# Four PSUM banks in place of two for the block products of the last second-layer stage

## The chip, the cores and the metric

The kernel runs on one core of one Trainium2 chip. TensorE (PE) multiplies and writes its results to the accumulation memory PSUM; the kernel's two pools there divide it into eight banks of 512 fp32 values in each of 128 partitions. In the part that matters, VectorE (DVE) and ScalarE (ACT) read PSUM, GpSimd (POOL) works on the memory SBUF, and SyncE (SP) issues the output stores. The metric is the device time of one execution in microseconds; three runs of the kernel before gave 546.70, 546.79 and 546.79, median 546.79.

## What is computed

```python
attn = np.maximum(q @ k.T * scale, 0) ** 2 / S       # 8 batches, 12 heads, 448 x 64
x    = (attn @ v), heads side by side                # 8 x 448 x 768
xn   = (x - mean(x)) / sqrt(var(x) + 1e-6) * g_ln
out  = x + maximum(xn @ w_ch1, 0) @ w_ch2            # w_ch1: 768 x 3072, w_ch2: 3072 x 768
```

Inputs and output are fp32; the kernel multiplies in bf16 and accumulates in fp32. The division by the square root is done at the very end: each row of the second layer's result is multiplied by its 1/sqrt and x is added.

## The kernel before, in words

The eight batches are worked in four pairs of two batches, that is 896 tokens or seven tiles of 128 tokens a pair. For the first three pairs attention of the next pair is interleaved with the two layers of this one. The program is written out in order by hand (`manual_schedule`, L74): each engine executes its instructions in the order in which the Python code issues them, and semaphores are put in for every dependence between engines. For the waits, the unit in PSUM is the tile that a pool hands out.

The change lies in the last stage alone: the second layer of the last pair (L854 to L859). Here the hidden activations `h` (`hT`, bf16, 24 chunks of 128 by 896) and the weights `w2` are treated as 2 x 2 blocks. The two rows of blocks of `h` are the token tiles t and t+4, its two columns the halves of the 24 chunks; the blocks of `w2` are the halves of its chunks by the halves of its 768 columns. Seven block products in place of eight give the four results (a scheme of Strassen's kind). A product (`product(n)`, L706) is 12 matmuls, each 128x128 weights by 128x384 moving data, accumulated in one PSUM bank. Its left factor is `s3` or `s4` (parts of `hT`) or one of the sums of blocks of `h` (`s2`, `s5`, `s1`, `s6`, `s7`: `h_sums_of`, L685), its right factor one of the sums of blocks of `w2`, made earlier.

`ffn2_pair` (L699) does one pair of tiles and is called for t = 0, 1, 2; `ffn2_last` (L760) then does tile 3 in the ordinary way: 24 matmuls into a bank for its first 384 columns and 24 into a bank for each of two groups of 192 columns. In `ffn2_pair`:

- the products come in the order 3, 2, 5, 4, 1, 6, 7. Products 3 and 2 start in fresh banks `a` and `b`; 5 adds to `a` and 4 adds to `b`. Products 1 and 6 start in fresh banks again, and 7 adds to that of product 1. A fresh bank is a one-bank tile from the pool `ps_mm` (L90), which has two buffers; so product 1 uses the bank that 3 and 5 had, and 6 the bank of 2 and 4;
- between the products the intermediate values are read: ACT copies `a` to `d` (L733), DVE subtracts `b` from `d` (L735), ACT copies the sums `c12` (L738) and `c21` (L742), DVE makes `q_ = a + d` (L745), POOL takes `c12` from `d` and adds `c21` (L746, L747), DVE adds `b` to `q_` (L752) and the last `a` to `d` (L757);
- `result` (L720) multiplies a result by 1/sqrt and adds x, on DVE in one instruction (L724) or on ACT (L727) and POOL (L728), and issues two stores on SP (L645);
- `following` (L855) issues the sums of `h` for the next t on DVE: `s2` and `s5` in one instruction (L691), `s1` (L693), `s6` (L695) and `s7` (L697). For t = 2 it issues nothing.

On DVE the order for one t is then L735, L691, L745, L724 twice (`c12`, `c21`), L693, L752, L695, L697, L757, L724 (`d`). The other pool in PSUM, `ps_sc` (L89), has three buffers of two banks each, `[128, 2, 512]` fp32; it served attention and is idle in this stage.

Of the kernel before, what the change touches and what calls it, by code (L numbers as in the profile page):

```python
# [28 lines left out]
def kernel(  # L29
# [22 lines left out]
    nc = tc.nc  # L52
    P = 128
    HP = 64
    bf16 = mybir.dt.bfloat16
    fp32 = mybir.dt.float32
# [13 lines left out]
    DH = d_model // 2  # L70
# [18 lines left out]
    ps_sc = ctx.enter_context(tc.tile_pool(name="ps_sc", bufs=3, space=bass.MemoryType.PSUM))  # L89
    ps_mm = ctx.enter_context(tc.tile_pool(name="ps_mm", bufs=2, space=bass.MemoryType.PSUM))  # L90
# [550 lines left out]
    def store(pair, t, cols, o, queues):  # L641
        for u, queue in enumerate(queues):
            b, j = divmod(2 * t + u, J)
            rows = out[2 * pair + b].rearrange("(p j) d -> j p d", j=J)[j]
            queue.dma_start(rows[:, cols], o[u * HP:(u + 1) * HP])  # L645
# [39 lines left out]
    def h_sums_of(pair, t, names, lo, hi):  # L685

        h = hT[pair].rearrange("p (kh k) (u s) -> p kh k u s", kh=2, s=P)
        a = {(i, j): h[:, j, lo:hi, t + 4 * i] for i in range(2) for j in range(2)}
        if "s2" in names:
            two = [h[:, j, lo:hi, t:t + 5:4].rearrange("p k u s -> p u k s") for j in range(2)]  # L690
            nc.vector.tensor_add(h_sum["s25"][:, ::-1, lo:hi], *two)  # L691
        if "s1" in names:
            nc.vector.tensor_add(h_sum["s1"][:, lo:hi], a[0, 0], a[1, 1])  # L693
        if "s6" in names:
            nc.vector.tensor_sub(h_sum["s6"][:, lo:hi], a[1, 0], a[0, 0])  # L695
        if "s7" in names:
            nc.vector.tensor_sub(h_sum["s7"][:, lo:hi], a[0, 1], a[1, 1])  # L697

    def ffn2_pair(pair, t, late, following):  # L699


        h = hT[pair].rearrange("p (kh k) (u s) -> p kh k u s", kh=2, s=P)
        left = dict(h_sum, s3=h[:, 0, :, t], s4=h[:, 1, :, t + 4])
        left["s2"], left["s5"] = h_sum["s2"], h_sum["s5"]

        def product(n, ps=None):  # L706
            first = ps is None
            if first:
                ps = ps_mm.tile([P, 512], fp32, tag="mm", name="m_ps")
            x, y = left[f"s{n}"], w2_sum[f"t{n}"]  # L710
            for ki in range(KH):
                nc.tensor.matmul(ps[:, :DH], x[:, ki], y[:, ki],  # L712
                                 start=(first and ki == 0), stop=(ki == KH - 1),
                                 skip_group_check=not first)
            return ps

        def fp():
            return late.tile([P, DH], fp32, tag="z", name="z_sb", bufs=5)

        def result(eng, z, row, half):  # L720
            u = t + 4 * row
            z3, x = z.rearrange("p (c d) -> p c d", d=D), xtok[pair][:, :, u, half * HP:(half + 1) * HP]
            if eng is nc.vector:
                eng.scalar_tensor_tensor(  # L724
                    z3, z3, rstd[pair][:, u:u + 1], x, op0=ALU.mult, op1=ALU.add)
            else:
                nc.scalar.mul(z, z, rstd[pair][:, u:u + 1])  # L727
                eng.tensor_add(z3, z3, x)  # L728
            store(pair, u, slice(half * DH, (half + 1) * DH), z, (nc.sync, nc.sync))

        a = product(3)
        d = fp()
        nc.scalar.copy(d, a[:, :DH])  # L733
        b = product(2)
        nc.vector.tensor_sub(d, d, b[:, :DH])  # L735
        product(5, a)
        c12 = fp()
        nc.scalar.copy(c12, a[:, :DH])  # L738
        product(4, b)
        following("s2")  # L740
        c21 = fp()
        nc.scalar.copy(c21, b[:, :DH])  # L742
        a = product(1)
        q_ = fp()
        nc.vector.tensor_add(q_, a[:, :DH], d)  # L745
        nc.gpsimd.tensor_sub(d, d, c12)  # L746
        nc.gpsimd.tensor_add(d, d, c21)  # L747
        result(nc.vector, c12, 0, 1)
        result(nc.vector, c21, 1, 0)
        b = product(6)  # L750
        following("s1")
        nc.vector.tensor_add(q_, q_, b[:, :DH])  # L752
        result(nc.gpsimd, q_, 1, 1)
        product(7, a)
        following("s6")
        following("s7")
        nc.vector.tensor_add(d, d, a[:, :DH])  # L757
        result(nc.vector, d, 0, 0)

    def ffn2_last(pair, t):  # L760
# [93 lines left out]
    for t in range(3):  # L854
        def following(name, t=t):  # L855
            if t < 2:
                h_sums_of(pair, t + 1, (name,), 0, KH)
        ffn2_pair(pair, t, late, following)
# [31 lines left out]
```

## Time and profile before

| what | value |
|---|---|
| median of three runs | 546.79 us |
| the profiled execution | 546.87 us |
| its span, first to last instruction | 545.0 us |
| mean granted TensorE clock | 0.999 |
| PE busy, of the span | 533.3 us (98%) |
| DVE, ACT and POOL busy | 300.2, 267.9 and 119.6 us |
| first matmul of this stage (L712) starts | 487.69 us |
| first matmul of `ffn2_last` (L766) starts | 533.29 us |
| last instruction on DVE (L634) starts | 541.35 us |

A timeline view lists instructions in order of time: start, duration, engine, line, operation, output and inputs, how many were merged (`x12`), and in brackets how long the engine had been idle before and what ended that. A merged row of 12 matmuls is one product; `x24` is two products without a pause, `x36` three. A row of matmuls lasts until the modelled end of its last matmul, which is some 0.16 us after the next one may begin; so what matters is from start to start. The waits view gives, for each pair of waiter and releaser, the total in us, the number of times and the longest.

### The profile page before, as it was taken

Reading aid. Unit: us, or ns where it says so; the run is one execution under the profiler, and the core shown is the slowest. Engines: PE = TensorE matmul, PEld = TensorE weight load, DVE = VectorE, ACT = ScalarE, POOL = GpSimd, SP = SyncE. Lnnn points to the kernel's source line nnn. Section 1 sums busy time; section 2 is a strip of 40 time slices with the busy share of each in tenths; the row PEclk is TensorE's granted clock in tenths of the full one; section 3 lists DMA queues with packets and bytes.
Section 4 is the critical chain, followed back from the end, with each engine's and each line's share of the span. In section 5 each row is a group of like instructions: output and inputs, shape, how many; then the busy total and the mean of one; then the engine's idle time right before and its main releaser. Section 6 shows DMA issues by size and latency. Waiting matters only on the chain.

```text
span 545.0 us, 11195 instructions
## 1 busy us (share of the span) xinstructions
PE 533.3 (98%) x4720; PEld 315.5 (58%) x4720; DVE 300.2 (55%) x559; ACT 267.9 (49%) x440; POOL 119.6 (22%) x144
## 2 busy tenths in 40 slices
PE   8999999999999999999999999999999999999996
PEld 6677779655555555555555555555555555555555
DVE  5765752378886250057787432026687689035543
ACT  6967685555553444455545344445545244441110
POOL 7344111123526100003634400001230400001121
PEclk9999999999999999999999999999999999999999
DMA  9999999979999930029989980004831140001123
GB/s 197 206 205 208 211 171 185 168 126 160 164 152 146 167 42 1 0 55 147 163 149 134 176 109 1 1 14 88 151 75 31 44 102 1 1 0 26 34 58 88
DMA packets 111300, 56.64 MB, mean 104 GB/s; under 512 B 77330, under 2 KB 111250, under 8 KB 111250
## 3 DMA queue, kind: packets, MB, share of 16 engines
q0 software_dynamic: 26976, 25.50, 32.4%
q1 hardware_dynamic: 83490, 29.77, 31.8%
q8 instruction: 37, 0.61, 0.5%
q10 hardware_dynamic: 784, 0.66, 0.4%
q14 instruction: 13, 0.11, 0.1%
HBM read 51.91 MB, written 11.01 MB: 115 GB/s over the span
## 4 chain that ended last, share of the span: by engine, by line
PE 91%; DVE 2%; DMA 2%; POOL 2%; issue 1%; ACT 1%; POOLq 0%; DVEq 0%
PE h_ps L586 39%; PE o_ps L623 31%; PE sc_ps L331 7%; PE av_ps L361 6%; PE m_ps L712 5%; DMA w<-in_moe_w_ch_dram 2%; PE o_ps L766 1%; PE h_ps L608 1%; PE sum_ps L414 1%; DVE z_sb L724 1%; POOL z_sb L746 1%; ACT early L342 1%; PE tr_ps L216 0%; DVE h_sum L697 0%; POOL v_sb L126 0%
## 5 line engine op out<-in xcount | busy, mean ns | idle before, releaser
L586 PE MATMUL h_ps<-xc_sb,w 128*128 128x448 bf16 (+2 forms) x1368 | 218.9, 318 | 0.6 <-ACT early L342 0.3
L586 PEld LDWEIGHTS <-w 128*128 128x128 bf16 x1368 | 128.6, 98 | 86.6 <-issue 3.0
L623 PE MATMUL o_ps<-w,hT_sb 128*128 128x384 bf16 x1008 | 172.6, 326 | 0.0
L342 ACT ACTIVATE attn_sb<-sc_ps 128x896 bf16<-128x896 f32 (+4 forms) x150 | 126.4, 902 | 87.9 <-PE sc_ps L331 71.4
L594 ACT ACTIVATE hT_sb<-h_ps 128x448 bf16<-128x448 f32 (+2 forms) x213 | 103.0, 484 | 122.2 <-PE h_ps L586 121.7
L623 PEld LDWEIGHTS <-hT_sb 128*128 128x128 bf16 x1008 | 94.9, 98 | 74.7 <-issue 15.2
L344 DVE TENSOR_TENSOR attn_sb<-attn_sb 128x896 bf16<-128x896 bf16 x126 | 81.7, 654 | 40.2 <-ACT attn_sb L342 38.9
L565 DVE BATCH_NORM_STATS2 stats<-xtok_sb 128x6 f32<-128x384 bf16 x56 | 27.5, 533 | 34.3 <-DMA xtok_sb<-xT_sb 34.3
L397 POOL TENSOR_TENSOR part_sb<-part_sb,xT_sb 128x448 f32<-128x448 f32 x24 | 29.5, 1229 | 69.9 <-DVE xT_sb L368 62.3
L394 POOL TENSOR_TENSOR part_sb<-xT_sb 128x448 f32<-128x448 bf16 x6 | 6.6, 1105 | 172.9 <-DVE xT_sb L368 142.5
L571 DVE RECIPROCAL rstd_sb<-rstd_sb 128x1 f32<-128x1 f32 (+1 forms) x10 | 1.7, 168 | 72.4 <-ACT rstd_sb L570 72.4
L420 DVE SCALAR_TENSOR_TENSOR xc_sb<-total_sb,g_mean,xc_sb 128x448 bf16<-128x448 f32 (+2 forms) x54 | 29.0, 604 | 21.5 <-ACT total_sb L418 21.5
L634 DVE SCALAR_TENSOR_TENSOR o_sb<-o_ps,rstd_sb,xtok_sb 128x384 f32<-128x384 f32 (+1 forms) x45 | 27.0, 601 | 17.2 <-PE o_ps L623 11.0
L331 PE MATMUL sc_ps<-qT_sb,kT_sb 64*64 64x448 bf16 x504 | 35.0, 358 | 0.0
L368 DVE TENSOR_SCALAR xT_sb<-av_ps 128x896 bf16<-128x896 f32 (+2 forms) x30 | 27.0, 900 | 10.0 <-PE av_ps L361 9.8
L361 PE MATMUL av_ps<-attn_sb,v_sb 64*64 64x448 bf16 (+2 forms) x672 | 32.3, 327 | 0.0
L361 PEld LDWEIGHTS <-v_sb 64*64 64x64 bf16 x840 | 22.7, 107 | 11.9 <-issue 1.6
L384 DVE TENSOR_SCALAR xc_sb<-xT_sb,g_sb 128x448 bf16<-128x448 bf16 (+2 forms) x54 | 27.9, 567 | 1.0
L712 PEld LDWEIGHTS <-h_sum 128*128 128x128 bf16 x180 | 17.6, 98 | 12.9 <-issue 1.4
L331 PEld LDWEIGHTS <-kT_sb 64*64 64x64 bf16 x504 | 12.1, 105 | 17.6 <-issue 13.3
L126 POOL DMA_DIRECT2D v_sb<-in_v_dram x24 | 17.5, 730 | 20.2 <-PE av_ps L361 16.7
L746 POOL TENSOR_TENSOR z_sb<-z_sb 128x384 f32<-128x384 f32 x3 | 3.0, 998 | 81.7 <-DVE z_sb L745 81.7
(88 smaller groups left out, 335.8 us busy)
## 6 DMA issues: line engine op xcount, KB each, us to landing
out_dram<-o_sb SPq DMA_DIRECT2D x85, 96.0 KB, 3.0
v_sb<-in_v_dram POOLq DMA_DIRECT2D x24, 224.0 KB, 4.9
w<-in_moe_w_ch_dram POOLq DMA_DIRECT2D x12, 384.0 KB, 13.9
w<-in_moe_w_ch_dram POOLq DMA_DIRECT2D x4, 1152.0 KB, 20.0
q_sb<-in_q_dram POOLq DMA_DIRECT2D x20, 224.0 KB, 7.0
k_sb<-in_k_dram POOLq DMA_DIRECT2D x20, 224.0 KB, 5.7
out_dram<-z_sb SPq DMA_DIRECT2D x24, 96.0 KB, 2.2
hold_sb<-in_q_dram POOLq DMA_DIRECT2D x3, 224.0 KB, 11.9
```

Source lines behind the costliest of these rows:

```text
L331: nc.tensor.matmul(ps[cols, r, o * w:(o + 1) * w], g["k"](i)[rows, cols], g["q"](i, r)[rows, blk[0]:sum(blk), cols], start=True, stop=True)
L342: nc.scalar.activation(a, ps[:, :, :len(slots) * w], ACTF.Relu)
L344: nc.vector.tensor_mul(a, a, a)
L361: nc.tensor.matmul(ps[cols, hh, :w], v_sb[rows, pr, j * D:(j + 1) * D], g["attn"][i][rows, r, :], start=(j == 0), stop=(j == J - 1))
L384: nc.vector.tensor_scalar_mul(y, x, g_sb[:, c:c + 1])
L397: nc.gpsimd.tensor_add(part[b], part[b], x[:, c])
L420: nc.vector.scalar_tensor_tensor(xc[b][:, c, of(blk)], total, g_mean[:, c:c + 1], xc[b][:, c, of(blk)], op0=ALU.mult, op1=ALU.add)
L565: nc.vector.bn_stats(stats[:, n], xtok[pair][:, n * G:(n + 1) * G, t, :])
L586: nc.tensor.matmul(ps[:, :w], w1[:, c, ni * P:(ni + 1) * P], xc[b][:, c, of(blk)], start=(c == 0), stop=(c == K1 - 1))
L594: nc.scalar.activation(hT[pair][:, ni, o:o + w], ps[:, :w], ACTF.Relu)
L623: nc.tensor.matmul(ps[:, :DH], hT[pair][:, ki, t * P:(t + 1) * P], w2[:, ki, cols], start=(ki == 0), stop=(ki == K2 - 1))
L712: nc.tensor.matmul(ps[:, :DH], x[:, ki], y[:, ki], start=(first and ki == 0), stop=(ki == KH - 1), skip_group_check=not first)
```

## The change

The products' banks come from `ps_sc`: `banks()` takes one two-bank tile and hands out its halves as `a` and `b`. Each call of `ffn2_pair` takes two such tiles, the first for products 3, 2, 5 and 4, the second for 1, 6 and 7. The order of the products is the same. On DVE, the sums of `h` and the reads of banks move ahead of the results: after the change the order is L736 (was L735), L691, L747 (was L745), L693, L752, L695, L724 twice, L758 (was L757), L697, L724. The stores of `q_` are issued ahead of those of `c12` and `c21`. All lines below L705 shift by one or two.

```diff
-        def product(n, ps=None):
-            first = ps is None
-            if first:
-                ps = ps_mm.tile([P, 512], fp32, tag="mm", name="m_ps")
+        def banks():
+            two = ps_sc.tile([P, 2, 512], fp32, tag="sc", name="m_ps")
+            return two[:, 0, :DH], two[:, 1, :DH]
+
+        def product(n, ps, first=True):
             x, y = left[f"s{n}"], w2_sum[f"t{n}"]
             for ki in range(KH):
-                nc.tensor.matmul(ps[:, :DH], x[:, ki], y[:, ki],
+                nc.tensor.matmul(ps, x[:, ki], y[:, ki],
                                  start=(first and ki == 0), stop=(ki == KH - 1),
                                  skip_group_check=not first)
-            return ps
...
-        a = product(3)
+        a, b = banks()
+        product(3, a)
         d = fp()
-        nc.scalar.copy(d, a[:, :DH])
-        b = product(2)
-        nc.vector.tensor_sub(d, d, b[:, :DH])
-        product(5, a)
+        nc.scalar.copy(d, a)
+        product(2, b)
+        nc.vector.tensor_sub(d, d, b)
+        product(5, a, False)
         c12 = fp()
-        nc.scalar.copy(c12, a[:, :DH])
-        product(4, b)
+        nc.scalar.copy(c12, a)
+        product(4, b, False)
         following("s2")
         c21 = fp()
-        nc.scalar.copy(c21, b[:, :DH])
-        a = product(1)
+        nc.scalar.copy(c21, b)
+        a, b = banks()
+        product(1, a)
         q_ = fp()
-        nc.vector.tensor_add(q_, a[:, :DH], d)
+        nc.vector.tensor_add(q_, a, d)
         nc.gpsimd.tensor_sub(d, d, c12)
         nc.gpsimd.tensor_add(d, d, c21)
+        following("s1")
+        product(6, b)
+        nc.vector.tensor_add(q_, q_, b)
+        result(nc.gpsimd, q_, 1, 1)
+        following("s6")
         result(nc.vector, c12, 0, 1)
         result(nc.vector, c21, 1, 0)
-        b = product(6)
-        following("s1")
-        nc.vector.tensor_add(q_, q_, b[:, :DH])
-        result(nc.gpsimd, q_, 1, 1)
-        product(7, a)
-        following("s6")
+        product(7, a, False)
+        nc.vector.tensor_add(d, d, a)
         following("s7")
-        nc.vector.tensor_add(d, d, a[:, :DH])
         result(nc.vector, d, 0, 0)
```

## The prediction, written before the changed kernel ran

> **What bounds the kernel now.** I read the page first: it says which engine has no room.
>
> ```profile
> span 545.0 us, 11195 instructions
> PE 533.3 (98%) x4720; PEld 315.5 (58%) x4720; DVE 300.2 (55%) x559; ACT 267.9 (49%) x440; POOL 119.6 (22%) x144
> ```
>
> PE is the bound over the whole span, so only what makes PE wait, or stop waiting, can move the time. The second view is the list of waits, for PE alone, from 487 us on, where the changed lines run.
>
> ```profile
> PE m_ps L712 <- DVE z_sb L752: 2.5, 2, 1.3
> PE m_ps L712 <- DVE z_sb L757: 0.8, 1, 0.8
> PE o_ps L766 <- DVE z_sb L752: 0.4, 1, 0.4
> ```
>
> PE waits four times here, always for DVE to finish reading a bank (a fifth, short one shows below). The third view is the timeline of PE alone over the stage; the start of each row is what counts.
>
> ```profile
> 487.69 2.11 PE L712 MATMUL m_ps<-w_sum,hT_sb 128*128 128x384 bf16 x12
> 489.64 4.06 PE L712 MATMUL m_ps<-w,h_sum 128*128 128x384 bf16 x24
> 493.54 2.11 PE L712 MATMUL m_ps<-w_sum,hT_sb 128*128 128x384 bf16 x12
> 495.49 6.01 PE L712 MATMUL m_ps<-w_sum,h_sum 128*128 128x384 bf16 x36
> 502.74 2.11 PE L712 MATMUL m_ps<-w_sum,hT_sb 128*128 128x384 bf16 x12 [1.23 <-DVE z_sb L752]
> 505.66 4.06 PE L712 MATMUL m_ps<-w,h_sum 128*128 128x384 bf16 x24 [0.81 <-DVE z_sb L757]
> 509.55 2.11 PE L712 MATMUL m_ps<-w_sum,hT_sb 128*128 128x384 bf16 x12
> 511.50 6.01 PE L712 MATMUL m_ps<-w_sum,h_sum 128*128 128x384 bf16 x36
> 518.81 2.11 PE L712 MATMUL m_ps<-w_sum,hT_sb 128*128 128x384 bf16 x12 [1.29 <-DVE z_sb L752]
> 521.01 4.06 PE L712 MATMUL m_ps<-w,h_sum 128*128 128x384 bf16 x24
> 526.86 6.01 PE L712 MATMUL m_ps<-w_sum,h_sum 128*128 128x384 bf16 x36
> 533.29 8.02 PE L766 MATMUL o_ps<-w,hT_sb 128*128 128x384 bf16 x72 [0.42 <-DVE z_sb L752]
> ```
>
> A product that nothing holds up takes 1.95 us from start to start (487.69 to 489.64; 509.55 to 511.50), and the seven of one t run without a pause. The pauses lie between one t and the next. The fourth view is the timeline of all engines: when a bank's reader starts after a product.
>
> ```profile
> 504.88 0.48 ACT L733 COPY z_sb<-m_ps 128x384 f32<-128x384 f32 x1 [1.55 <-PE m_ps L712]
> 507.87 0.56 DVE L735 TENSOR_TENSOR z_sb<-z_sb,m_ps 128x384 f32<-128x384 f32 x1 [1.61 <-PE m_ps L712]
> 509.80 0.48 ACT L738 COPY z_sb<-m_ps 128x384 f32<-128x384 f32 x1 [4.43 <-PE m_ps L712]
> 513.71 0.56 DVE L745 TENSOR_TENSOR z_sb<-m_ps,z_sb 128x384 f32<-128x384 f32 x1 [2.20 <-PE m_ps L712]
> ```
>
> Product 3 starts at 502.74 and its reader, ACT's copy, at 504.88: 2.14 us later, more than the 1.95 after which PE could go on. So whenever the next product must await the reader of this one, PE loses the difference, the reader's own time and the release.
>
> **The change part by part.**
>
> *Removed: the waits between one t and the next.* With two one-bank buffers product 3 of the next t writes the bank that L752 read, and product 2 the bank that L757 read; both reads stand on DVE behind L724 and the sums of h. After the change these two products have a fresh two-bank tile out of three; its earlier readers were done a whole t before, and o_ps finds ps_mm empty. Loss now, from start to start: after three products from 495.49 (5.84 us) product 3 could start at 501.33 and starts at 502.74, 1.41; product 2 at 504.69 against 505.66, 0.97; then 517.34 against 518.81, 1.47; 520.76 against 521.01, 0.25; and o_ps at 532.70 against 533.29, 0.59. Sum **4.69 us removed**. The new order on DVE (bank reads and sums ahead of L724) would shorten the same waits; with fresh banks it has nothing left to gain, and I count it at nothing.
>
> *Added: waits inside each t.* The diff alone doesn't tell this; the order of the changed program's instructions with their waits does. For t = 1, the first matmul of each product (3, 2, 5, 4, 1, 6, 7, and then 3 of t = 2):
>
> ```
> 8956 L713 Matmult m_ps_6736<-w2_sum_6153,hT_sb_6154 128x384
> 8980 L713 Matmult m_ps_6736<-w2_971,h_sum_6546 128x384 [waits Activation_49]
> 9004 L713 Matmult m_ps_6736<-w2_971,h_sum_6546 128x384 [waits DVE_49]
> 9028 L713 Matmult m_ps_6736<-w2_sum_6153,hT_sb_6154 128x384 [waits Activation_49]
> 9052 L713 Matmult m_ps_6793<-w2_sum_6153,h_sum_6546 128x384
> 9076 L713 Matmult m_ps_6793<-w2_sum_6153,h_sum1_6547 128x384 [waits DVE_49]
> 9100 L713 Matmult m_ps_6793<-w2_sum_6153,h_sum1_6548 128x384 [waits DVE_49]
> 9124 L713 Matmult m_ps_6852<-w2_sum_6153,hT_sb_6154 128x384
> ```
>
> Both banks are one tile (m_ps_6736) now. Product 2 goes into a bank that nobody has used for a whole t, and yet waits for ACT: the semaphore's count is the one that L734 raises, ACT's copy of the *other* bank. In the same way 5 awaits DVE's read of b (L736), 4 ACT's copy of a (L739), 6 DVE's read of a (L747) and 7 DVE's read of b (L752). The dependence is kept by tile, and each of these readers reads the product just before. So five of the seven products start only when their predecessor has been finished, read out and released. Behind each waiting matmul stands all the rest of PE's queue, and nothing else bounds the end.
>
> The price of each is start to reader, plus the reader, plus the release, less 1.95. The release of PE by DVE: L752 ends at 502.14 + 0.54 = 502.68 and PE starts at 502.74, 0.06. By ACT no row of this stage has it; the nearest is at the kernel's start, where a copy (L342) ends at 12.63 and PE starts at 12.65: 0.02, and another there gives about 0.11. I take 0.05, near DVE's 0.06.
> - 3 to 2: 2.14 (504.88 - 502.74) + 0.48 + 0.05 - 1.95 = 0.72.
> - 2 to 5: 2.21 (507.87 - 505.66) + 0.56 + 0.06 - 1.95 = 0.88.
> - 5 to 4: product 5 starts 1.95 after 505.66, at 507.61; 2.19 (509.80 - 507.61) + 0.48 + 0.05 - 1.95 = 0.77.
> - 1 to 6: 2.21 (513.71 - 511.50) + 0.56 + 0.06 - 1.95 = 0.88.
> - 6 to 7: L752 never follows its product at once now, as L724 is ahead of it; with the readers' 2.14 to 2.21, so 2.18, + 0.54 + 0.06 - 1.95 = 0.83.
>
> Sum 4.08 a t, and three t: **12.2 us added**. From the ends of the rows (ACT's release 0.02 or 0.11; start to reader 2.14 or 2.22) a t costs 3.8 to 4.3, so 11.5 to 12.9.
>
> *Covers.* The price holds if the reader is free when its product ends. DVE's next reader is L747, behind L691 (1.76 us), which starts when product 5 ends; products 4 and 1 then take over 4 us. L752 stands behind L693 (0.87), beside product 6 (2.15). L736 of the next t stands behind L695, L724 twice, L758, L697 and L724; after product 7 only L758 (0.54), L697 (0.87) and L724 (0.62) are left, 2.0 us, beside products 3 and 2 of the next t, 4.8 us. ACT's L739 awaits a buffer that is stored behind L752, L727 (0.62) and L728 (1 to 1.7) of the t before, and such a store lands 2.2 us (median) after its issue: some 5 us after L752, while L739 comes over 9 us after it. If such a cover were gone, PE would wait the excess, once per t. L724's results come some 2 us later and the stores on SP in another order: nothing but the buffers awaits them. The tail after o_ps (541.32 to the end) is as before.
>
> **Sum.** The profiled execution took 546.87 us, 1.87 more than its span; it lies 0.08 above the median of the runs. + 12.2 - 4.7 = + 7.5 us: 546.79 + 7.5 = **554.3 us**, 1.4% slower.
>
> **The rivals.**
>
> *The added waits do not bite* (each bank waits for its own readers only). Then true dependences remain: 5 must await the copy of a, ready 2.7 us after product 3 starts, needed after 3.9; 4 and 7 likewise. Nothing stalls, only the 4.7 us go: 546.79 - 4.7 = 542.1, faster. For it: in the trace of before product 2 starts at 489.64 and writes its bank while ACT reads the other from 489.89, without a pause. It decides if what 8980 awaits were an older count of ACT than the copy's. Against it: the count is that of the copy just before, the same pattern stands in all three t, and fresh tiles (8956, 9052) have no wait at all. Chance 4%. The Trainium skill, PSUM — Partial Sum Buffer, section "PSUM bank collisions raise a hardware error", states that two engines on different banks run clean; by that the chip asks for none of the five waits, and the time would be this rival's 542.1. The trace agrees about the chip, at 489.64 and 489.89; but the waits are in the program, and PE executes them.
>
> *The clock falls.* Fifteen pauses of 0.8 us might let the granted clock drop. If one product of seven then ran at half speed, 1.95 us more per t, 5.9: 560.2. Against it: 1.41 us and 0.97 us lost within 4 us before 505.66 left the next 24 matmuls at 3.89 us, and the granted clock of the windows from 487.4 to 532.6 is 1.00. Chance 3%. The Trainium skill, TensorE: Matmul & The Clock Gate, section "A second HAM failure mode: psum-queue depth-cycling", tells of a kernel whose short idle times between groups in PSUM brought the clock down again and again; by it this rival would be the forecast, and no row here bears it out.
>
> **How the numbers follow.** Forecast 92%, no waits 4%, clock 3%; 1% that part of the hand-off is hidden and gain and loss cancel within 0.2%, which is about what a measurement of this kernel can tell from no change. Slower 95%, the same 1%, faster 4%. The range: + 11.5 - 4.7 gives 553.6, + 12.9 - 4.7 gives 555.0; 0.6 below and 1.0 above for the row that is not measured by itself (L752) and what a cover may cost: 553.0 to 556.0. The rivals lie outside, 8%.
>
> **What would show it.** Right: five pauses on PE in each t, 0.7 to 0.9 us each from start to start, ended by ACT L734 and L739 and by DVE L736, L747 and L752; none before product 1, before product 3 of the next t and before o_ps. PE's last matmul some 7.5 us later than before. Wrong: x36 rows without a pause in a t (first rival), or rows of 12 matmuls longer than 2.11 (second).

## The result, and the profile after

Four runs of the changed kernel gave 553.92 to 554.40 us, median 554.24, against 546.75 of four runs before: ratio 1.0137, interval 1.0119 to 1.0155. It is slower by 7.5 us. The profiled execution took 554.22 us, its span is 552.4, 7.4 longer than before. In four of the sets of runs below, and in one set of the kernel before, one run lies about 3 us above the others; the ratios take it in, the medians hardly do, so the text goes by medians.

The list of waits of PE from 487 us on, in the kernel after (waiter, releaser: us in total, times, longest):

```profile
PE m_ps L713 <- DVE z_sb L736: 2.1, 3, 0.7
PE m_ps L713 <- DVE z_sb L747: 1.9, 3, 0.6
PE m_ps L713 <- DVE z_sb L752: 1.9, 3, 0.6
PE m_ps L713 <- ACT z_sb L739: 1.8, 3, 0.6
PE m_ps L713 <- ACT z_sb L734: 1.7, 3, 0.6
```

The four waits of before are gone and five others are there, each once in each of the three t. The timeline of PE in the same kernel, for the second t and the start of the third, and the first row of `ffn2_last`:

```profile
505.46 2.11 PE L713 MATMUL m_ps<-w_sum,hT_sb 128*128 128x384 bf16 x12
508.14 2.11 PE L713 MATMUL m_ps<-w,h_sum 128*128 128x384 bf16 x12 [0.57 <-ACT z_sb L734]
510.97 2.11 PE L713 MATMUL m_ps<-w,h_sum 128*128 128x384 bf16 x12 [0.71 <-DVE z_sb L736]
513.69 2.11 PE L713 MATMUL m_ps<-w_sum,hT_sb 128*128 128x384 bf16 x12 [0.61 <-ACT z_sb L739]
515.63 2.11 PE L713 MATMUL m_ps<-w_sum,h_sum 128*128 128x384 bf16 x12
518.40 2.11 PE L713 MATMUL m_ps<-w_sum,h_sum 128*128 128x384 bf16 x12 [0.65 <-DVE z_sb L747]
521.15 2.11 PE L713 MATMUL m_ps<-w_sum,h_sum 128*128 128x384 bf16 x12 [0.64 <-DVE z_sb L752]
523.10 2.11 PE L713 MATMUL m_ps<-w_sum,hT_sb 128*128 128x384 bf16 x12
...
540.72 8.02 PE L768 MATMUL o_ps<-w,hT_sb 128*128 128x384 bf16 x72
```

The rows of 24 and 36 matmuls have fallen apart into single products. Products 3 (505.46, 523.10) and 1 (515.63) follow without a pause, as does `o_ps`; the other five each begin 2.7 to 2.8 us after the product before. From 487.83 to 540.72 the 21 products took 52.9 us where 21 x 1.95 = 40.9 would do: 11.9 lost. Before it was 45.6 (487.69 to 533.29), 4.7 lost. The difference of 7.3 us, and 0.14 by which the stage began later, is the whole of the 7.4.

### The profile page after: what moved, and what is told of

Read it like the earlier page. It is cut to its first block, busy times and chain, and to the rows that moved or that the text cites. A ratio compares the mean times of both kernels' runs of the same rounds, so it can differ in the third digit from the quotient of the medians.

```text
span 552.4 us, 11193 instructions
## 1 busy us (share of the span) xinstructions
PE 535.3 (97%) x4720; PEld 315.6 (57%) x4720; DVE 298.6 (54%) x559; ACT 267.9 (48%) x440; POOL 119.5 (22%) x144
## 4 chain that ended last, share of the span: by engine, by line
PE 93%; DMA 2%; POOL 1%; ACT 1%; DVE 1%; issue 1%; ACTq 0%; DVEq 0%; POOLq 0%
PE h_ps L586 39%; PE o_ps L623 31%; PE m_ps L713 8%; PE sc_ps L331 7%; PE av_ps L361 6%; DMA w<-in_moe_w_ch_dram 2%; PE o_ps L768 1%; PE h_ps L608 1%; PE sum_ps L414 1%; ACT early L342 1%; PE tr_ps L216 0%; POOL v_sb L126 0%; POOL w L144 0%; DVE z_sb L747 0%; DVE z_sb L752 0%
## 5 line engine op out<-in xcount | busy, mean ns | idle before, releaser
L342 ACT ACTIVATE attn_sb<-sc_ps 128x896 bf16<-128x896 f32 (+4 forms) x150 | 126.3, 902 | 87.4 <-PE sc_ps L331 70.9
L748 POOL TENSOR_TENSOR z_sb<-z_sb 128x384 f32<-128x384 f32 x3 | 4.2, 1385 | 92.2 <-DVE z_sb L747 92.2
L713 PE MATMUL m_ps<-w_sum,h_sum 128*128 128x384 bf16 x108 | 19.0, 326 | 3.9 <-DVE z_sb L747 1.9
L331 PEld LDWEIGHTS <-kT_sb 64*64 64x64 bf16 x504 | 12.1, 105 | 17.6 <-issue 13.3
## 6 DMA issues: line engine op xcount, KB each, us to landing
hold_sb<-in_q_dram POOLq DMA_DIRECT2D x3, 224.0 KB, 11.9
```

The costliest lines, as they stand in the source:

```text
L331: nc.tensor.matmul(ps[cols, r, o * w:(o + 1) * w], g["k"](i)[rows, cols], g["q"](i, r)[rows, blk[0]:sum(blk), cols], start=True, stop=True)
L342: nc.scalar.activation(a, ps[:, :, :len(slots) * w], ACTF.Relu)
L713: nc.tensor.matmul(ps, x[:, ki], y[:, ki], start=(first and ki == 0), stop=(ki == KH - 1), skip_group_check=not first)
```

## The experiments

The theory is the prediction's: dependences in PSUM are kept by tile, and with two banks in a tile a product awaits the reader of the product just before. Rivals are that the chip itself holds a product up while another bank is read, that two-bank tiles cost as such, and that the order on DVE matters by itself. Of the seven kernels below, the first, second, fourth and sixth stand beside eleven runs of the kernel before (median 546.81), the third and the seventh beside thirteen on another chip (546.83), the fifth beside ten (546.89).

**Four banks, each in its own tile** (the same order on every engine as in the changed kernel):

```diff
         def banks():
-            two = ps_sc.tile([P, 2, 512], fp32, tag="sc", name="m_ps")
-            return two[:, 0, :DH], two[:, 1, :DH]
+            a = ps_sc.tile([P, 2, 512], fp32, tag="sc", name="m_ps")
+            b = ps_mm.tile([P, 512], fp32, tag="mm", name="n_ps")
+            return a[:, 0, :DH], b[:, :DH]
```

> The changed kernel with a and b in tiles of their own (a from ps_sc, b from ps_mm): four banks as before, the same order on every engine. Theory, that the five waits a t come from two banks sharing a tile: all fifteen pauses go, PE runs from 488 us to its last matmul without one, 554.2 - 12.1 (measured loss from start to start in the changed kernel) = 542.2 us, 4.6 under the kernel before. Rival, that a product into a bank is held up on the chip itself while another bank is read: the pauses stay, 554 us.

Measured: 542.18 us. PE's timeline in this kernel, the last three products of the first t, the first of the next and `ffn2_last`:

```profile
495.51 2.11 PE L714 MATMUL m_ps<-w_sum,h_sum 128*128 128x384 bf16 x12
497.46 2.11 PE L714 MATMUL n_ps<-w_sum,h_sum 128*128 128x384 bf16 x12
499.41 2.11 PE L714 MATMUL m_ps<-w_sum,h_sum 128*128 128x384 bf16 x12
501.36 2.11 PE L714 MATMUL m_ps<-w_sum,hT_sb 128*128 128x384 bf16 x12
...
528.66 8.02 PE L769 MATMUL o_ps<-w,hT_sb 128*128 128x384 bf16 x72
```

Every product starts 1.95 us after the one before, across the boundary between two t as well (499.41 to 501.36). The expectation's 12.1 is a little more than the 11.9 of the rows above, by which it would have been 542.3. The reads of the other bank still lie beside the matmuls, and cost nothing; product 2 and ACT's read of product 3, in the same kernel:

```profile
489.66 2.11 PE L714 MATMUL n_ps<-w,h_sum 128*128 128x384 bf16 x12
489.90 0.48 ACT L735 COPY z_sb<-m_ps 128x384 f32<-128x384 f32 x1 [1.45 <-PE m_ps L714]
```

So the waits were the shared tile's, and the rival of contention on the chip falls. One form of it is not tried by this kernel, nor by the next: that only the two banks of one two-bank tile disturb each other. Against it stand the semaphores in the program's list of waits, and that in the first t of the changed kernel each paused product starts 0.05 to 0.06 us after the end of just the reader that its semaphore names (ACT's L734 ends at 490.50, product 2 starts at 490.55).

**Crossed tiles**: two-bank tiles again, but `a` from one and `b` from the other.

```diff
-        a, b = banks()
+        (a, a2), (b, b2) = banks(), banks()
         product(3, a)
...
-        a, b = banks()
+        a, b = a2, b2
         product(1, a)
```

> The changed kernel with both two-bank tiles of a t taken at its start, a being the first half of each and b of the second tile: products 3, 5, 1, 7 in one tile, 2, 4, 6 in the other. Two banks still share a tile and dependences are still kept by tile, but a matmul never awaits the reader of the product just before, only that of the one before it. Theory, that what costs is waiting for the reader of the predecessor: a reader is done 2.7 to 2.8 us after its product starts and is needed after 3.9, so no pause, 542.2 us. Rival, that two-bank tiles as such cost (their layout, or readers that are slower on them): 550 to 554 us.

Measured: 542.20 us. PE's timeline for the first t, and the first row of the second:

```profile
487.67 2.11 PE L713 MATMUL m_ps<-w_sum,hT_sb 128*128 128x384 bf16 x12
489.62 4.06 PE L713 MATMUL m_ps<-w,h_sum 128*128 128x384 bf16 x24
493.52 2.11 PE L713 MATMUL m_ps<-w_sum,hT_sb 128*128 128x384 bf16 x12
495.47 6.01 PE L713 MATMUL m_ps<-w_sum,h_sum 128*128 128x384 bf16 x36
501.32 2.11 PE L713 MATMUL m_ps<-w_sum,hT_sb 128*128 128x384 bf16 x12
```

The x24 and x36 rows are back. Nothing differs from the changed kernel but which of the four banks share a tile. By the rule of the tile, product 1 must still await ACT's copy (L739) out of its tile's other bank; but that copy reads product 5, not product 4, and it ends at 494.20, before product 1 can start at 495.47. A wait that is over in time leaves no row in the trace, so this one is inferred from the rule. A false dependence costs only where the awaited reader is later than the waiter.

**Half of it**: the first four products in tiles of their own, 1, 6 and 7 in a shared one.

```diff
-        a, b = banks()
+        a, b = own()          # as banks() of the first experiment
         product(3, a)
```

> The changed kernel, but products 3, 2, 5 and 4 in tiles of their own and only 1, 6 and 7 in a shared tile. Theory: three of the five pauses a t go (0.75, 0.88 and 0.76 us by the changed kernel's trace), two stay (0.82 and 0.81): 554.2 - 7.2 = 547.0 us. Rivals: if the pauses hide one another, so that the rest grow when some go, 550 us or more; if sharing costs nothing, 542.

Measured: 547.14 us (0.1% above the 546.83 beside it; ratio 1.0011, 1.0000 to 1.0023). PE's waits in this kernel:

```profile
PE m_ps L718 <- DVE z_sb L752: 1.9, 3, 0.6
PE m_ps L718 <- DVE z_sb L757: 1.9, 3, 0.6
```

Two pauses a t are left, of the same length as before: the pauses add, and none hides another. That this kernel takes as long as the kernel before is a coincidence of 4.9 us lost inside the t against 4.7 between them.

**The order on DVE alone**, with the two one-bank buffers of the kernel before (the moves of `following` and `result` in the change's diff, and nothing of `banks`):

> The kernel before with its two one-bank buffers and only the new order on DVE. Theory: L752 follows product 6 at once, so product 3 of the next t and o_ps don't wait; product 2 of the next t still awaits the read of product 7's bank behind L724 twice, 0 to 0.3 us twice. 546.75 - 4.7 + 0 to 0.6 = 542.1 to 542.7 us. Rival, that the order is worth nothing and only fresh banks take away the pauses: 546.7 us.

Measured: 543.66 us, ratio to before 0.9953 (0.9937 to 0.9969): the rival falls, but the time is 1.0 us above the upper end of what was expected. PE waits twice for L756, the read of product 7's bank. DVE between the first and the second t in this kernel, and POOL at the same time:

```profile
500.02 1.75 DVE L695 TENSOR_TENSOR h_sum<-hT_sb 128x1536 bf16<-128x1536 bf16 x1
501.69 1.79 DVE L724 SCALAR_TENSOR_TENSOR z_sb<-z_sb,rstd_sb,xtok_sb 128x384 f32<-128x384 f32 x2
503.40 0.54 DVE L756 TENSOR_TENSOR z_sb<-z_sb,m_ps 128x384 f32<-128x384 f32 x1
```

```profile
499.95 1.00 POOL L747 TENSOR_TENSOR z_sb<-z_sb 128x384 f32<-128x384 f32 x1
500.90 1.63 POOL L728 TENSOR_TENSOR z_sb<-z_sb,xtok_sb 128x384 f32<-128x384 f32 x1
```

L695 takes 1.75 us here and 0.94 in the kernel before; it starts at 500.02, while POOL's L747 runs until 500.95, and ends 0.82 after that, at 501.77. POOL's L728 then starts at 500.90 and takes 1.63, where 0.91 is its time in the first t of the kernel before; it ends 0.76 after L695. The two engines seem to have taken turns. So L756 ends at 503.94, product 2 starts at 504.00 in place of 503.24 (501.29 + 1.95), 0.76 lost, twice.

**The read first**: as the last kernel, with the two `result` calls on DVE moved behind the read of product 7.

```diff
-        result(nc.vector, c12, 0, 1)
-        result(nc.vector, c21, 1, 0)
         product(7, a)
         nc.vector.tensor_add(d, d, a[:, :DH])
+        result(nc.vector, c12, 0, 1)
+        result(nc.vector, c21, 1, 0)
```

> The kernel with the new order on DVE and the two one-bank buffers of the kernel before, in which product 2 of the next t still lost 0.76 us twice; here the two results on DVE (L724) also stand behind the read of product 7's bank. Theory, that the loss came from that read standing on DVE behind L695 (1.75 us there in place of 0.9, beside POOL's additions) and L724 twice (1.79 us): without L724 ahead it is done before product 2 needs the bank, no pause is left, 543.7 - 1.5 = 542.2 us, with two banks only. Rival, that two banks are too few whatever the order: 543.7 us.

Measured: 542.24 us beside 546.89, ratio 0.9916 (0.9903 to 0.9930), and no wait of PE in the stage. L695 still takes 1.75 us there; the read now ends at 502.21, a microsecond before product 2 needs the bank at 503.23. Two banks suffice here. DVE's read of product 7 and PE's next product 2 in this kernel:

```profile
501.67 0.54 DVE L754 TENSOR_TENSOR z_sb<-z_sb,m_ps 128x384 f32<-128x384 f32 x1
503.23 4.06 PE L712 MATMUL m_ps<-w,h_sum 128*128 128x384 bf16 x24
```

**Four banks of their own with the old order on DVE** (the first experiment's `banks`, the order of the kernel before):

> Four banks in tiles of their own and the order on DVE of the kernel before: the banks' half of the change alone, without the shared tile. Theory, as the prediction had it, that with fresh banks the order has nothing to gain: 542.1 us, as the same banks with the new order. Rival, that DVE's late reads still hold up PE somewhere: 1 to 4 us more.

Measured: 542.10 us, ratio 0.9915 (0.9902 to 0.9927), no pause on PE. With banks to spare the order has nothing to gain, and with the order of the kernel just above (the read first) the banks have nothing.

**Shared tiles with the old order on DVE** (the changed kernel's `banks`, the order of the kernel before):

> The changed kernel's two-bank tiles with the order on DVE of the kernel before. Theory: product 7 now awaits L752, and L752 stands on DVE behind L724 twice and L693; by the trace of before it ends 4.48 us after L745 starts (498.20 end of L745, 502.68 end of L752), so product 7 starts some 4.5 us after product 6 in place of 2.76 in the first two t, and some 3.6 us in the third, where L693 is missing: 2 x 1.7 + 0.9 = 4.3 us more than the changed kernel, 558.6 us. Rival, the prediction's word that the order has nothing to gain: 554.2 us.

Measured: 559.21 us (four runs, from 558.57 to 559.99), ratio 1.0231 (1.0214 to 1.0248); the profiled execution took 558.61. The expectation's 4.48 us counts from the end of L745, when product 6 may start, and not from its start; product 7 does start 4.48 us after product 6 (505.21 - 500.73). One row of the waits of PE, and DVE in the first t, in this kernel:

```profile
PE m_ps L713 <- DVE z_sb L754: 6.2, 3, 2.4
```

```profile
500.12 0.56 DVE L747 TENSOR_TENSOR z_sb<-m_ps,z_sb 128x384 f32<-128x384 f32 x1 [2.87 <-PE m_ps L713]
501.84 1.98 DVE L724 SCALAR_TENSOR_TENSOR z_sb<-z_sb,rstd_sb,xtok_sb 128x384 f32<-128x384 f32 x2 [1.16 <-POOL z_sb L748]
503.75 0.94 DVE L693 TENSOR_TENSOR h_sum<-hT_sb 128x1536 bf16<-128x1536 bf16 x1
504.61 0.54 DVE L754 TENSOR_TENSOR z_sb<-z_sb,m_ps 128x384 f32<-128x384 f32 x1
```

L754 is the addition that is L752 in the changed kernel. It reads product 6, which started at 500.73 and was done by 502.9; but it stands on DVE behind L724, which awaits POOL, and L693. So the wait for it is 2.4 us in place of 0.6 (1.5 in the third t, which has no L693). The new order saved the changed kernel 4.4 us of what the shared tile would have cost by the two profiled executions (558.61 against 554.22), 5.0 by the medians.

The best versions, 542.1 to 542.2 us, are 0.85% under the kernel before. What is left on PE in this stage is matmuls from end to end.

## Why the prediction was right

- *The sum.* Predicted 554.3, measured 554.24. Added 12.2 against 11.9 measured, removed 4.69 against 4.7 (all of it: no wait is left between one t and the next in the kernel after). That the two times agree within 0.1 us is in part luck: the added sum was 0.3 too high, and 0.14 of that was made up by the later start of the stage (487.83 against 487.69), which no term foresaw.
- *The five terms*, mean of three t from start to start, less 1.95: 3 to 2 0.74 (predicted 0.72), 2 to 5 0.87 (0.88), 5 to 4 0.75 (0.77), 1 to 6 0.81 (0.88), 6 to 7 0.80 (0.83). The largest miss is 0.07, in 1 to 6: L747 starts 2.15 us after its product in each t (500.15 - 498.00 in the first) and not 2.21. The release by ACT, a price without a row of this stage, was taken at 0.05, from an activation (L342, which the prediction calls a copy) at the kernel's start: in the kernel after L734 ends at 490.02 + 0.48 = 490.50 and PE starts at 490.55, 0.05.
- *The step that was wrong*: "The new order on DVE ... with fresh banks it has nothing to gain, and I count it at nothing." That is true of fresh banks in tiles of their own (542.18 and 542.10), but not of the shared tile, where product 7 awaits L752 and the order decides when L752 runs: 4.4 to 5.0 us. The number did not suffer, because the terms were worked out on the new order; a reader who undid the order as worthless would have lost them.
- *The rival that the waits do not bite* was half of the truth: its 542.1 is the time that the chip needs once the program leaves the waits out (542.18). The Trainium skill, PSUM — Partial Sum Buffer, section "PSUM bank collisions raise a hardware error", holds that engines on different banks run clean; the runs agree, and the 11.9 us were the program's own waits.
- *The rival of the clock* did not come. Fifteen pauses, and the granted clock was 1.00 in each third of the stage (487.8 to 540.7), every product 2.11 us. The Trainium skill, TensorE: Matmul & The Clock Gate, section "A second HAM failure mode: psum-queue depth-cycling", tells of a kernel in which short idle times made it fall; pauses of 0.57 to 0.71 us did not do that here.

## What to carry to other kernels

Two buffers that are written in turn belong in two tiles, or in halves of tiles that are not used one after the other: where dependences are kept by tile, a shared tile makes each writer await its predecessor's reader, and the price is start to reader, plus reader, plus release, less the spacing (here 0.74 to 0.87 us a time). Such waits are not in the diff; look at the semaphores in front of the first instruction of each group, and at what raises them. And before adding banks, see whether the late reader merely stands behind other work on its own engine: moving it forward was worth as much here as two more banks.

## What the runs showed of the hardware

DVE and POOL seem to take turns on SBUF, as far as POOL's spans, which are rough in the profile, let one tell. A sum of `h` on DVE (two bf16 inputs, 128x1536) took 0.94 us alone and 1.75 when POOL's addition was running as it started, and POOL's addition behind it 1.63 in place of 0.91. The Trainium skill, SBUF — State Buffer, section "Who interferes with whom", says that a DVE instruction with two SBUF inputs contends with a GpSimd instruction that reads SBUF, and that the contention is an exclusive lock; the trace agrees: DVE's 501.77 is 0.82 after POOL's end at 500.95, nearly the 0.94 of the whole instruction. The kernel before had shown the same pair already, in its first t:

```profile
502.61 0.94 DVE L695 TENSOR_TENSOR h_sum<-hT_sb 128x1536 bf16<-128x1536 bf16 x1
503.41 0.91 POOL L728 TENSOR_TENSOR z_sb<-z_sb,xtok_sb 128x384 f32<-128x384 f32 x1 [3.01 <-ACT z_sb L727]
503.48 1.66 DVE L697 TENSOR_TENSOR h_sum<-hT_sb 128x1536 bf16<-128x1536 bf16 x1
```

L697, a sum of the same size as L695, starts while L728 runs and takes 1.66. This was left out of what was expected of the order on DVE alone: without the 0.81 us, and with all else unchanged, L756 would by this estimate have ended at 503.13, before product 2 needs the bank at 503.24.
